# Experts' remainders in halves and quarters of a block: 19 steps a phase for 20

## The chip, the cores and the metric

One core of one Trainium2 chip. The metric is the device time of one execution in microseconds (us); the kernel before takes 680.72 us, the median of three runs.

## The reference

Two stages, one after the other. Attention: 4 batches, 8 heads, 1152 keys of 64 numbers; pairs of queries are averaged, so 576 rows a head. Its output, 4 x 576 = 2304 tokens of 512 numbers, goes through a mixture of eight experts, of which each token uses one:

```python
logits = np.einsum('bsd,de->bse', x, w_gate)
local_gate = 1.0 / (1.0 + np.exp(-np.einsum('bsd,de->bse', x, w_local).squeeze(-1)))
...
            fresh_e = int(np.argmax(logits[b, s]))
            if s == 0 or local_gate[b, s] < 0.5:
                e = fresh_e
            else:
                e = prev_e if prev_e >= 0 else fresh_e
...
            h = np.maximum(x[b, s] @ w1[e], 0.0)
            out[b, s] = p[e] * (h @ w2[e])
```

w1 is 512 x 1024 and w2 1024 x 512 for each expert; p is the softmax of the token's logits. How many tokens an expert gets depends on the data.

## The kernel before, in words

Attention runs over 32 heads until about 422 us; the change does not touch it. The gate of the last batch and the routing follow, and then the experts.

**Blocks.** Tokens are sorted by expert into blocks of 128. A phase has `NST` = 20 steps, one block each. 16 of them hold tokens of one expert (whole blocks). The four of `PAIRS` = (7, 11, 15, 19) hold two halves of 64 tokens, each with an expert of its own: the part of an expert's tokens that is left over its whole blocks goes into a half if it is at most 64, else into a whole block. `positions` (L1045) gives a pair two positions, j and one from 25 on. Where more than 16 whole blocks are needed, five further blocks are computed by `tail` (L1226) behind a branch.

**Phases.** There are eight: w1's quarter q in phase 2q (`mm1`, `block1`), w2's quarter q in phase 2q + 1 (`mm2`, `block2`). All numbers are split into a high and a low half of 16 bits, so each product is three matmuls. W[0] and W[1] hold the current quarter of w1 and of w2 for all eight experts. While a phase runs, the other one's W is filled for the next phase: 16 pieces, each loaded by SP (`w_load`, 256 KB), its high half made by ScalarE (`w_hi`, L586), its low half by VectorE (`w_lo`, L592). In step j of phases 1 to 6 the load of piece c goes out at j = 14c // 15, the high half three steps later, the low half four. Seven buffers hold loads.

**mm1.** The stationary operand is a 128 x 128 piece of the block's weights, the moving one the 128 tokens; a whole block has 24 matmuls of 128 columns, a pair 48 of 64. Since the expert is known only at run time, its 512 KB of weights (128 x 2048) are copied out of W first (`copy`, L1048): by VectorE into one of three `wc` buffers, or by a DMA of SP into one of three `wd` buffers (`DMAC` names the step and the position). VectorE's copies are issued one step ahead, SP's four steps ahead but never across a phase. The result goes through ScalarE (L1071: relu, high half of h) and VectorE (L1072: low half of h).

**mm2.** The stationary operand is h, the moving one 512 columns of the expert's weights, read in W[1] itself through a register; a whole block has 6 matmuls. A pair writes its halves to PSUM partitions 0 to 63 and 64 to 127 by 12 matmuls on 64 columns of the array each; the second half's weights come from a `wd` copy. In phase 1 ScalarE takes the result into `acc` (L1125), later VectorE adds to it (L1129), and in phase 7 GpSimd scatters each block's rows to the output (L1220).

**The order of work** is written out by hand: the instructions of each engine run in the program's order, and `experts` (L1100) issues, step by step, the copies, in phase 0 the gathers and transposes of later blocks, the halves of W, then the matmuls. SP's queue has the loads and the wd copies in that one order.

**Routing.** The first six blocks (`NF`) are settled from three batches and computed for phase 0 while the last batch is routed. Then `route_ops` (s1 to s9, L881 to L957) does some 25 small operations on VectorE: counts, a running sum over the experts, block and row of each token; 40 matmuls (L934, L936) turn them into lists of token numbers, by which GpSimd gathers the blocks (L1019). The list `rest` (L785) weaves these with the gate's and with the first blocks' work (`PLAN`).

```python
DMAC = {5: 0, 7: 1, 9: 0, 11: 1, 13: 0, 15: 1, 17: 0, 19: 1}
...
        elif DMAC.get(j) == k and ph:
            w, src, eng = self.wd.tile([128, 2048], F16, name="wd", tag="wd"), self.es[c], self.nc.sync.dma_start
...
            copy_to(byd, min(i + 4, ph * NST + NST - 1))
            copy_to(byv, min(i + 1, ph * NST + NST - 1))
```

Of the kernel before, what the change touches and what calls it, by code (L numbers as in the profile page):

```python
# [442 lines left out]
NBLK = 25  # L443
NST = 20
PAIRS = (7, 11, 15, 19)
NFULL = NST - len(PAIRS)
NCOL = NBLK + len(PAIRS)
PST = slice(PAIRS[0], NST, 4)
NG = 20
# [17 lines left out]
DMAC = {5: 0, 7: 1, 9: 0, 11: 1, 13: 0, 15: 1, 17: 0, 19: 1}  # L467
# [4 lines left out]
def consts():  # L472
# [7 lines left out]
    full = [j for j in range(NBLK) if j not in PAIRS]  # L480
    key = np.zeros(NCOL)
    key[full] = np.arange(len(full))
    key[list(PAIRS) + list(range(NBLK, NCOL))] = len(full) + np.arange(2 * len(PAIRS))
    a[:, 384:384 + NCOL] = key[None]
    c["c16"] = a
    f = np.zeros((128, 113), np.float32)
    f[:, 0:8] = 8 - np.arange(8)
    f[:, 8:16] = np.arange(8)
    f[:, 16:32] = 1
    f[:, 24] = 0  # L490
    f[:, 34:59] = np.where(np.isin(np.arange(NBLK), PAIRS), 99, key[:NBLK])
    f[:, 60:85] = 4000 + np.arange(128)[:, None] * 25 + np.arange(25)[None]
# [23 lines left out]
class Moe:  # L516
    def __init__(self, tc, ctx, cc, io, out):
# [12 lines left out]
        self.c32 = per.tile([128, 113], F32, name="c32")  # L530
# [12 lines left out]
        self.eji = per.tile([128, NCOL], I32, name="eji")  # L543
# [7 lines left out]
        self.ejf = per.tile([128, NCOL], F32, name="ejf")  # L551
# [43 lines left out]
    def gate_ops(self, b, XR, xT, sml, psum, ptag, wide):  # L595
# [199 lines left out]
    def full_ops(self, sml, psum, ptag):  # L795
# [76 lines left out]
    def route_ops(self):  # L872
# [8 lines left out]
        def s1():  # L881
# [6 lines left out]
            st["ni"], st["en"] = w[:, 216:232].bitcast(I32), w[:, 232:248]  # L888
            st["s3"] = w[:, 248:308].rearrange("p (g v) -> p g v", v=3)
            st["jf"], st["c"] = w[:, 308:328], w[:, 328:348]  # L890
            V.tensor_scalar(out=st["ni"][:, 0:8], in0=self.cy, scalar1=63.0, scalar2=None, op0=ALU.add)
            V.tensor_scalar(out=st["ni"][:, 8:16], in0=self.cy, scalar1=127.0, scalar2=None, op0=ALU.add)

        def s2():
            V.tensor_scalar(out=st["ni"], in0=st["ni"], scalar1=7, scalar2=None, op0=ALU.arith_shift_right)
            V.tensor_copy(st["vec"][:, 8:24], st["ni"])
            V.tensor_tensor(out=st["vec"][:, 16:24], in0=st["vec"][:, 16:24], in1=st["vec"][:, 8:16], op=ALU.subtract)

        def s3():
# [22 lines left out]
        def s8(psum, ptag):  # L922
# [9 lines left out]
            for h in (1, 0):  # L932
                for g in range(h * hg, h * hg + hg):
                    T.matmul(p2, self.R[:, g], jj[:, g, :, 0:n], start=(g == hg), stop=False, skip_group_check=True)  # L934
                for g in range(h * hg, h * hg + hg):
                    T.matmul(p2[64:128, :, PAIRS[0] - NF:NST - NF:4], self.R[:, g, 0:64], jj[:, g, :, n:nc_], start=False, stop=(g == hg - 1), skip_group_check=True)  # L936
            ge, ej = w[:, 0:8 * n].rearrange("p (j e) -> p j e", e=8), self.ejf[:, NF:NBLK]
            gh, eh = w[:, 152:216].rearrange("p (j e) -> p j e", e=8), st["c"][:, 0:8]
            V.tensor_tensor(out=ge, in0=c32[:, 34 + NF:59].unsqueeze(2).to_broadcast(bj), in1=en[:, 0:8].unsqueeze(1).to_broadcast(bj), op=ALU.is_ge)
            V.tensor_tensor(out=gh, in0=c32[:, 8:16].unsqueeze(2).to_broadcast(be), in1=en[:, 8:16].unsqueeze(1).to_broadcast(be), op=ALU.is_ge)  # L940
            V.tensor_reduce(out=ej.unsqueeze(2), in_=ge, op=ALU.add, axis=AX.X)
            V.tensor_reduce(out=eh.unsqueeze(2), in_=gh, op=ALU.add, axis=AX.X)

        def s9():
            pi, en, w = st["pi"], st["en"], st["w2"]
            ej, t1, eh = self.ejf[:, NF:NBLK], self.cnt, st["c"][:, 0:8]
            V.tensor_scalar(out=self.gid[:, NF:], in0=pi[:, n:2 * n], scalar1=1152.0, scalar2=None, op0=ALU.add)
            V.tensor_tensor(out=ej, in0=ej, in1=self.E1[:, NF:], op=ALU.add)
            V.tensor_copy(self.ejf[:, PST], eh[:, 0:4])
            V.tensor_copy(self.ejf[:, NBLK:], eh[:, 4:8])  # L950
# [3 lines left out]

            V.tensor_copy(self.nbi, en[:, 7:8])
# [4 lines left out]
            def b0():  # L960
                V.tensor_copy(self.ejf[64:128, PST], self.ejf[64:128, NBLK:])
# [431 lines left out]
```

## Time and profile before

| | |
|---|---|
| runs | 680.72 us median (679.49 to 680.77, three runs) |
| the profiled execution | 675.04 us, of which the span is 672.9 |
| TensorE (PE) | 642.0 us busy, 95% of the span |
| VectorE (DVE) | 552.1 us, 82% |
| ScalarE (ACT) | 428.1 us, 64% |
| GpSimd (POOL) | 421.4 us, 63% |
| mean granted TensorE clock | 0.984 of 2.4 GHz |
| moved by DMA | 128.80 MB, 191 GB/s over the span |

Start times in rows count from the span's start; the phases begin at 447.67 (phase 0, from its seventh block), 474.88, 501.68, 528.77, 555.57, 582.67, 609.46 and 636.56 us. A busy share is an average over a stretch, and what a stage waits for is read in that stage. PE is the matmuls, PEld the loads of their stationary operand, SPq the queue on which SP issues DMAs: a row of it shows the issue, not the transfer. Matmul rows show a duration longer than the distance of two starts, since matmuls overlap in the array; the distance is what one costs.

### The profile page before, as it was taken

How to read it: one execution, taken by the hardware profiler on the slowest of the kernel's cores; microseconds unless marked ns; L12 is line 12 of the kernel's file. 1: busy time of each engine (PE TensorE's matmuls, PEld its weight loads, DVE VectorE, ACT ScalarE, POOL GpSimd, SP SyncE). 2: the span in 40 equal slices, each digit the busy share in tenths (PEclk: the TensorE clock that was granted, in tenths of full speed). 3: DMA queues.
4: the chain of work that ended last, by engine and by line, in shares of the span. 5: the costliest groups of instructions: out<-in, count | busy, mean ns of one | idle time of the engine just before them, and what ended most of it. 6: DMA issues, size and time to landing. Idle time of an engine off the chain costs nothing.

```text
span 672.9 us, 22880 instructions
## 1 busy us (share of the span) xinstructions
PE 642.0 (95%) x9247; PEld 499.0 (74%) x9247; DVE 552.1 (82%) x1045; ACT 428.1 (64%) x846; POOL 421.4 (63%) x383
## 2 busy tenths in 40 slices
PE   7999999999999999999999998789999999999994
PEld 2587888888888888878887787679559649848941
DVE  7788897897998888898888897759559899899852
ACT  3678778777778677778677565559776535544500
POOL 8899999998898998898998758166000000000064
PEclk9899999999999999999999999789999999999998
DMA  8864654667474578473684307678669769777763
GB/s 245 198 173 148 201 152 111 188 163 161 140 220 113 164 180 160 139 241 90 200 181 126 108 2 133 222 236 255 208 232 325 260 237 304 287 266 260 268 235 121
DMA packets 83228, 128.80 MB, mean 191 GB/s; under 512 B 35759, under 2 KB 42031, under 8 KB 83120
## 3 DMA queue, kind: packets, MB, share of 16 engines
q1 hardware_dynamic: 79920, 117.24, 58.7%
q0 software_dynamic: 3200, 10.05, 4.3%
q8 instruction: 76, 1.25, 0.7%
q14 instruction: 32, 0.26, 0.1%
HBM read 68.82 MB, written 10.04 MB: 117 GB/s over the span
## 4 chain that ended last, share of the span: by engine, by line
PE 51%; issue 29%; DVE 10%; POOL 4%; ACT 2%; DMA 2%; another core or an unknown queue 0%; SPq 0%; POOLq 0%; DVEq 0%; ACTq 0%
PE sc L268 9%; PE sc L270 8%; PE psm L242 7%; PE av L308 6%; PE av L311 5%; PE av L310 5%; PE av L312 4%; DVE mx L244 4%; POOL out L1220 3%; DVE pl L284 2%; PE psh L257 1%; PE psh L1205 1%; PE psm L240 1%; DMA xT<-xr 1%; DVE w L592 1%
## 5 line engine op out<-in xcount | busy, mean ns | idle before, releaser
L272 ACT ACTIVATE ph<-sc 128x576 f32<-128x576 f32 x288 | 186.9, 652 | 91.8 <-PE sc L270 72.9
L244 DVE TENSOR_REDUCE mx<-psm 128x1 f32<-128x512 f32 (+1 forms) x300 | 194.1, 663 | 44.4 <-PE psm L242 41.0
L284 POOL TENSOR_TENSOR pl<-ph 128x576 f16<-128x576 f32 x167 | 207.1, 1256 | 9.0 <-ACT ph L272 9.0
L312 PE MATMUL av<-vt,pl 128*128 128x65 f16 x1235 | 138.2, 192 | 1.1 <-issue 1.1
L311 PE MATMUL av<-vt,ph 128*128 128x64 f16 x1235 | 139.1, 195 | 0.0
L310 PE MATMUL av<-vt,ph 128*128 128x65 f16 x1235 | 138.6, 193 | 0.0
L311 PEld LDWEIGHTS <-ph 128*128 128x128 bf16 x1235 | 115.3, 97 | 20.6 <-issue 0.3
L1220 POOL DMA_INDIRECT out<-acc,sid x14 | 13.7, 979 | 177.6 <-DVE acc L1129 175.4
L310 PEld LDWEIGHTS <-ph 128*128 128x128 bf16 x1235 | 116.4, 97 | 10.9 <-issue 2.9
L268 PE MATMUL sc<-qs,ks 128*128 128x288 f16 x576 | 118.0, 286 | 2.8 <-DVE st L718 1.0
L270 PE MATMUL sc<-qa,ks 65*128 65x288 f16 (+1 forms) x576 | 118.1, 286 | 0.6 <-ACT qa L258 0.6
L312 PEld LDWEIGHTS <-pl 128*128 128x128 f16 x1235 | 115.7, 99 | 1.3 <-issue 1.3
L1216 PE MATMUL pso<-w,hq 128*128 x480 | 107.4, 380 | 0.0
L592 DVE SCALAR_TENSOR_TENSOR w<-wf,w 128x512 f16<-128x512 f32 x124 | 94.3, 765 | 13.1 <-ACT w L586 12.8
L1205 PEld LDWEIGHTS <-wc 128*128 128x128 f16 x1728 | 89.2, 99 | 7.2 <-issue 6.6
L1216 PEld LDWEIGHTS <-hq 128*128 128x128 f16 (+1 forms) x576 | 45.8, 102 | 59.8 <-issue 11.7
L586 ACT ACTIVATE w<-wf 128x512 f16<-128x512 f32 x124 | 76.4, 626 | 18.0 <-DMA wf<-wq 17.8
L1205 PE MATMUL psh<-xr,wc 128*128 128x128 f16 (+1 forms) x1584 | 85.0, 212 | 1.5 <-ACT xr L1034 0.7
L242 PE MATMUL psm<-ks,qs 128*128 128x512 f16 x232 | 83.2, 379 | 0.6 <-DVE mx L244 0.6
L284 DVE TENSOR_TENSOR pl<-ph 128x576 f16<-128x576 f32 x80 | 82.4, 1030 | 1.2 <-issue 1.2
L270 PEld LDWEIGHTS <-ks 65*128 65x128 f16 (+1 forms) x576 | 56.5, 98 | 15.4 <-issue 0.8
L1071 ACT ACTIVATE hq<-psh 128x256 f16<-128x256 f32 x74 | 28.4, 384 | 52.4 <-PE psh L1205 51.6
(241 smaller groups left out, 1014.5 us busy)
## 6 DMA issues: line engine op xcount, KB each, us to landing
wf<-wq SPq DMA_DIRECT2D x124, 256.0 KB
wd<-w SPq DMA_DIRECT2D x40, 512.0 KB
ks<-kd SPq DMA_DIRECT2D x32, 288.0 KB
vf<-vL SPq DMA_DIRECT2D x16, 576.0 KB
qf<-qeo SPq DMA_DIRECT2D x15, 576.0 KB
kf<-kT SPq DMA_DIRECT2D x14, 576.0 KB
qs<-qh SPq DMA_DIRECT2D x60, 72.0 KB
ks<-kl SPq DMA_DIRECT2D x30, 144.0 KB
```

Of the source, the lines that this page charges most:

```text
L242: T.matmul(m[:, 0:w], q[:, t * 128:t * 128 + 128], k[:, c * 512:c * 512 + w], start=True, stop=True)
L244: V.tensor_reduce(out=mx[:, i, c:c + 1], in_=m[:, 0:w], op=ALU.max, axis=AX.X)
L268: T.matmul(sc[:, c, 0:288], ksl, QS[p][:, j, c * 288:(c + 1) * 288], start=True, stop=False)
L270: T.matmul(sc[:, c, 0:288], kal, QA[p % 3][u, j, c * 288:(c + 1) * 288], start=False, stop=True)
L272: A.activation(out=PHI[g % NPH][:, r * Q:(r + 1) * Q].rearrange("p (c q) -> p c q", c=2), in_=sc[:, :, 0:288], func=AF.Exp, scale=1.0 / 16)
L284: x.tensor_tensor(out=PLO[g % NPH][:, r * Q:r * Q + Q], in0=pf, in1=top(pf), op=ALU.subtract)
L310: T.matmul(o, ph[:, c:c + 128], v[:, j, kt, 0:65], start=(kt == 0 and t == 0), stop=False, skip_group_check=True)
L311: T.matmul(o[:, 0:64], ph[:, c:c + 128], v[:, j, kt, 65:129], start=False, stop=False, skip_group_check=True)
L312: T.matmul(o, pl[:, c:c + 128], v[:, j, kt, 0:65], start=False, stop=(kt == NKT - 1 and t == 4), skip_group_check=True)
L592: self.nc.vector.scalar_tensor_tensor(out=lo, in0=t, scalar=float(2 ** (W2S if ph % 2 else W1S)), in1=hi, op0=ALU.mult, op1=ALU.subtract)
L1205: self.nc.tensor.matmul(p[:, ft, c], u[:, ws, kk, ft * 128:ft * 128 + 128], x[:, 2 * kk + xs_, c], start=(n == 0 and ft == 0 and i == 0), ...
L1216: self.nc.tensor.matmul(p[c], h(hs, ft)[:, c], u(ws, ft), start=(first and n == 0), stop=(last and n == e), skip_group_check=(m < 128))
```

## The change

Halves are joined by quarters. A phase has 19 steps: 16 whole blocks, two of halves (8 and 13) and one of four quarters (18). A remainder up to 32 tokens goes into a quarter, one up to 64 into a half, and what finds no room among four halves and four quarters into a whole block. The step of quarters has four positions, so 96 matmuls of 32 columns in mm1 and 24 on 32 columns of the array in mm2. The routing gets a third rounding, a longer scan, and 80 matmuls more for the quarters' lists. `DMAC` is a list now, with three of the quarters' four weight copies by DMA, in phase 0 too, so a first-matrix phase has eight copies by DMA as before (three in phase 0, where it had none), a second-matrix phase five for four; VectorE still copies 16 times in phases 2, 4 and 6.

```diff
-NBLK = 25
-NST = 20
-PAIRS = (7, 11, 15, 19)
-NFULL = NST - len(PAIRS)
-NCOL = NBLK + len(PAIRS)
+NBLK = 24
+NST = 19
+PAIRS = (8, 13)
+QUAD = 18
+SPEC = PAIRS + (QUAD,)
+NFULL = NST - len(SPEC)
+NCOL = NBLK + 6
...
-DMAC = {5: 0, 7: 1, 9: 0, 11: 1, 13: 0, 15: 1, 17: 0, 19: 1}
+DMAC = ((4, 0), (6, 0), (8, 1), (10, 0), (13, 1), (18, 1), (18, 2), (18, 3))
...
-            V.tensor_scalar(out=st["ni"][:, 0:8], in0=self.cy, scalar1=63.0, scalar2=None, op0=ALU.add)
-            V.tensor_scalar(out=st["ni"][:, 8:16], in0=self.cy, scalar1=127.0, scalar2=None, op0=ALU.add)
+            V.tensor_tensor(out=st["ni"].rearrange("p (v e) -> p v e", v=3), in0=self.cy.unsqueeze(1).to_broadcast([128, 3, 8]),
+                            in1=c32[:, 114:138].rearrange("p (v e) -> p v e", v=3), op=ALU.add)
...
-            V.tensor_tensor_scan(out=st["en"], data0=c32[:, 16:32], data1=st["vec"][:, 8:24], initial=self.F, op0=ALU.mult, op1=ALU.add)
+            hq, es, ov = st["hq"][:, 9:26], st["es"][:, 0:17], st["ov"]
+            V.tensor_tensor_scan(out=es, data0=c32[:, 16:33], data1=hq, initial=0.0, op0=ALU.mult, op1=ALU.add)
+            V.scalar_tensor_tensor(out=ov[:, 9:26], in0=es, scalar=4.75, in1=hq, op0=ALU.is_gt, op1=ALU.mult)
+            V.tensor_reduce(out=st["vec"][:, 8:16].unsqueeze(2), in_=ov.rearrange("p (v e) -> p e v", v=3)[:, 0:8], op=ALU.add, axis=AX.X)
+            V.tensor_tensor_scan(out=st["en"], data0=c32[:, 85:93], data1=st["vec"][:, 8:16], initial=self.F, op0=ALU.mult, op1=ALU.add)
...
+            for g in range(NG):
+                for c in range(4):
+                    T.matmul(pq[32 * c:32 * c + 32, 0:2], self.R[:, g, 0:32], jj[:, g, :, n + 2 + c], start=(g == 0), stop=(g == NG - 1), skip_group_check=True)
...
+            V.tensor_scalar(out=self.gid[:, QUAD:QUAD + 1], in0=st["pq"][:, 1:2], scalar1=1152.0, scalar2=None, op0=ALU.add)
+            V.tensor_copy(t1[:, QUAD - NF:QUAD - NF + 1], st["pq"][:, 0:1])
             V.tensor_copy(self.nbi, en[:, 7:8])
...
-        return [j, NBLK + PAIRS.index(j)] if j in PAIRS else [j]
+        return [j, NBLK + PAIRS.index(j)] if j in PAIRS else [j, NBLK + 5, NBLK + 6, NBLK + 7] if j == QUAD else [j]
...
-        elif DMAC.get(j) == k and ph:
+        elif (j, k) in DMAC and (ph or j == QUAD):
...
-            if j in PAIRS:
-                wd = self.wcp.pop((i, 1))
-                w.append(lambda s, ft: wd[:, s * 1024 + ft * 512:s * 1024 + ft * 512 + 512])
+            for k in range(1, len(self.positions(j))):
+                wd = self.wcp.pop((i, k))
+                w.append(lambda s, ft, wd=wd: wd[:, s * 1024 + ft * 512:s * 1024 + ft * 512 + 512])
...
-        first = [NF - 2 + c if c < NE else NF + (c - NE) * 10 // 11 for c in range(16)]
+        first = [NF - 2 + c if c < NE else NF + (c - NE) * 9 // 11 for c in range(16)]
...
-        byd = [(i, k) for i, k in parts if i > NST and DMAC.get(i % NST) == k and (k or i // NST % 2 == 0)]
+        byd = [(i, k) for i, k in parts if (i > NST or i % NST == QUAD) and (i % NST, k) in DMAC and (k or i // NST % 2 == 0)]
```

## Rows read from the trace of the kernel before

**Rows 1.** Busy time by stretch: phases 0, 1, 2, 3, 4 and 7; x counts instructions.

```profile
core 0: us, PE busy (x) PEld busy (x) DVE busy (x) ACT busy (x) POOL busy (x), PEclk, DMA share, GB/s
447.67:474.88 27.21, 26.41 (x528) 25.69 (x528) 24.61 (x52) 23.62 (x40) 15.61 (x21) 0.95 0.67 205
474.88:501.68 26.80, 26.80 (x150) 11.44 (x147) 13.90 (x22) 21.50 (x36) 0.00 (x0) 1.00 0.66 228
501.68:528.77 27.09, 27.09 (x578) 27.09 (x577) 24.12 (x48) 16.31 (x36) 0.00 (x0) 1.00 0.93 320
528.77:555.57 26.80, 26.80 (x150) 11.42 (x147) 24.47 (x38) 10.02 (x17) 0.00 (x0) 1.00 0.69 235
555.57:582.67 27.10, 27.10 (x579) 27.10 (x578) 25.52 (x51) 15.64 (x35) 0.00 (x0) 1.00 0.90 313
636.56:663.40 26.84, 26.84 (x150) 11.41 (x146) 14.14 (x20) 0.38 (x1) 15.66 (x16) 1.00 0.57 218
```

**Rows 2.** Timeline of TensorE in phase 4: start, duration, line, operands, shape, count.

```profile
562.28 1.50 PE L1205 MATMUL psh<-xr,wd 128*128 128x128 f16 x24
563.62 1.85 PE L1205 MATMUL psh<-xr,wc 128*128 128x128 f16 x36
...
566.36 1.50 PE L1205 MATMUL psh<-xr,wc 128*128 128x128 f16 x24
```

**Rows 3.** The gate's matmuls: the source line L661 (ns min/median/max), and its timeline.

```profile
L661 PE MATMUL wide<-wgh,xT x120: 167/169/184, 159.4 to 353.3; 128*128 128x18 f16 x60, 128*128 128x9 f16 x60
...
159.44 1.15 PE L661 MATMUL wide<-wgh,xT 128*128 128x18 f16 x40
```

**Rows 4.** Timeline of TensorE in phases 1 and 3.

```profile
474.88 5.34 PE L1216 MATMUL pso<-w,hq 128*128 x24
...
538.17 0.38 PE L1216 MATMUL pso<-w,hq 128*64 x1
538.17 0.38 PE L1216 MATMUL pso<-wd,hq 128*64 128x512 f16 x1
...
539.35 4.39 PE L1216 MATMUL pso<-w,hq 128*128 x19
...
544.76 4.39 PE L1216 MATMUL pso<-w,hq 128*128 x19
```

**Rows 5.** Timeline of phase 2: VectorE, and TensorE's weight load of step 16.

```profile
522.59 0.70 DVE L1062 COPY wc<-w 128x2048 f16 x1
...
523.34 1.34 PEld L1205 LDWEIGHTS <-wc 128*128 128x128 f16 x24
...
524.12 0.70 DVE L592 SCALAR_TENSOR_TENSOR w<-wf,w 128x512 f16<-128x512 f32 x1
```

**Rows 6.** SP's queue: issues around phases 2 and 4, and what they waited for.

```profile
SPq L1062 <- DVE w L592: 32.1, 6, 6.4
...
499.77 0.49 SPq L1062 DMA_DIRECT2D wd<-w  x1
...
509.92 0.49 SPq L1062 DMA_DIRECT2D wd<-w  x1
...
553.08 0.49 SPq L1062 DMA_DIRECT2D wd<-w  x1
```

**Rows 7.** Timeline of ScalarE: the high half of piece 14, in phases 2 and 4.

```profile
524.63 0.63 ACT L586 ACTIVATE w<-wf 128x512 f16<-128x512 f32 x1 [0.74 <-DMA wf<-wq]
...
577.87 0.63 ACT L586 ACTIVATE w<-wf 128x512 f16<-128x512 f32 x1
```

**Rows 8.** Timeline of the routing: VectorE and TensorE.

```profile
431.77 0.17 DVE L895 TENSOR_SCALAR wf<-wf 128x16 int32<-128x16 int32 x1
431.97 0.17 DVE L896 CAST wf<-wf 128x16 f32<-128x16 int32 x1
...
436.97 0.48 PE L936 MATMUL pi<-wf,R 128*64 128x8 f16 x10
...
442.44 1.38 PE L1205 MATMUL av<-xr,wc 128*128 128x128 f16 x19 [0.99 <-DVE wc L1062]
```

**Rows 9.** Timeline of GpSimd: the last scatter.

```profile
667.37 0.98 POOL L1220 DMA_INDIRECT out<-avf,sid  x1 [0.31 <-issue]
```

More of the change, by code (lines that the diff above doesn't have):

```diff
@@ L479, in consts @@
     a[:, 256:384] = 1
-    full = [j for j in range(NBLK) if j not in PAIRS]
-    key = np.zeros(NCOL)
+    full = [j for j in range(NBLK) if j not in SPEC]
+    key = np.full(NCOL, 999.0)
     key[full] = np.arange(len(full))
-    key[list(PAIRS) + list(range(NBLK, NCOL))] = len(full) + np.arange(2 * len(PAIRS))
+    key[list(PAIRS) + [NBLK, NBLK + 1]] = len(full) + np.arange(4)
+    key[NBLK + 2:] = len(full) + 0.5 + np.arange(4)
     a[:, 384:384 + NCOL] = key[None]
     c["c16"] = a
-    f = np.zeros((128, 113), np.float32)
+    f = np.zeros((128, 146), np.float32)
     f[:, 0:8] = 8 - np.arange(8)
     f[:, 8:16] = np.arange(8)
-    f[:, 16:32] = 1
+    f[:, 16:33] = 1
     f[:, 24] = 0
-    f[:, 34:59] = np.where(np.isin(np.arange(NBLK), PAIRS), 99, key[:NBLK])
-    f[:, 60:85] = 4000 + np.arange(128)[:, None] * 25 + np.arange(25)[None]
+    f[:, 34:34 + NBLK] = np.where(np.isin(np.arange(NBLK), SPEC), 99, key[:NBLK])
+    f[:, 60:60 + NBLK] = 4000 + np.arange(128)[:, None] * 25 + np.arange(NBLK)[None]
+    f[:, 114:138] = np.repeat([63, 95, 127], 8)[None]
+    f[:, 138:146] = np.array([2, 3, 0, 1, 0.5, 1.5, 2.5, 3.5])[None]
     f[:, 85:93] = 1
@@ L529, in __init__ @@
         self.c16 = con.tile([128, 640], F16, name="c16")
-        self.c32 = per.tile([128, 113], F32, name="c32")
+        self.c32 = per.tile([128, 146], F32, name="c32")
         self.wgf = con.tile([128, 4, 9], F32, name="wgf")
@@ L542, in __init__ @@
         self.sid = per.tile([128, NBLK], U32, name="sid")
-        self.eji = per.tile([128, NCOL], I32, name="eji")
+        self.eji = per.tile([128, NBLK + 8], I32, name="eji")
         self.nbi = per.tile([128, 1], I32, name="nbi")
@@ L550, in __init__ @@
         self.pall = per.tile([128, NST], F32, name="pall")
-        self.ejf = per.tile([128, NCOL], F32, name="ejf")
+        self.ejf = per.tile([128, NBLK + 8], F32, name="ejf")
         self.cnt = per.tile([128, NBLK - NF], F32, name="cnt")
@@ L932, in s8 @@
             for h in (1, 0):
[L933 removed]
+                gs = range(h * hg, h * hg + hg)
+                for g in gs:
                     T.matmul(p2, self.R[:, g], jj[:, g, :, 0:n], start=(g == hg), stop=False, skip_group_check=True)
[L935 to L936 removed]
+                for g in gs:
+                    T.matmul(p2[64:128, :, PAIRS[0] - NF:PAIRS[1] + 1 - NF:PAIRS[1] - PAIRS[0]], self.R[:, g, 0:64], jj[:, g, :, n:n + 2], start=False, stop=(g == hg - 1), skip_group_check=True)
```

62 lines of the change are left out of this document (36 added, 26 removed).

## The prediction

> **What bounds the kernel now.** I read the stretches first, since the change touches the routing (about 430 to 447 us) and the eight expert phases behind it. From 474.88 us on TensorE is busy for the whole of every stretch at a granted clock of 1.00 (2.4 GHz); in phase 0 it is busy 26.41 of 27.21 us [rows 1]. So a step that goes is worth what it holds of TensorE, if nothing else then decides. Two things nearly do, in the first-matrix phases (2, 4 and 6) alone: the DMA share is 0.93 and 0.90, and VectorE is busy 24.1 to 25.5 of 27.1 us. In the second-matrix phases (1, 3, 5, 7) the share is 0.66 to 0.69 and VectorE has room. The attention in front is not touched. The sum is made against the profiled execution (675.04 us, span 672.9); the median of the runs is 5.68 above it, no term below hangs on that, so the difference is taken from 680.72.
>
> **Does it compute the same blocks?** The experts get 192, 447, 145, 124, 34, 656, 132 and 574 tokens of the reference's inputs. Remainders over 64 go up to a whole block: 15 + 1 = 16 wholes, the old and the new limit. Before, 64, 63, 34, 62, 17, 16 and 4 are seven halves; after, the first four are halves (room for 4) and the last three quarters (room for 4). It fits exactly; no tail block runs.
>
> **TensorE's steps.** First matrix: a whole step runs from 562.28 to 563.62, 1.34; from 563.62 to 566.36 stand a whole and a pair, so the pair is 1.40 (48 matmuls of 64 columns, 29 ns each) [rows 2]. A step of quarters has 96 matmuls of 32 columns, each on a fresh 128x128 weight. No such row exists. Above stands 29 ns (2.80 us), below 32/64 of the pair's (1.40). Nearest is the gate's group of 9 and 18 columns with 128x128 weights: 40 in 1.15 us, the last one's 0.17 off, is 25 ns [rows 3]. I take 25: 2.41 us. Phase before: 16 x 1.34 + 4 x 1.40 = 27.1, as the stretch says; after: 21.46 + 2.80 + 2.41 = 26.7, a gain of only 0.4.
>
> Second matrix: 24 matmuls take 5.34, the last one's 0.38 off: 0.216 each, so a whole step of six is 1.29; three wholes and a pair take 544.76 - 539.35 = 5.41, so a pair is 1.53 [rows 4]. Its two halves start at the same 538.17: both column tiles run at once, and 0.24 goes at the change of shape. For four tiles I take the same, 1.53; bounds: 1.29, and if only two ran at once 12 x 0.216 + 0.24 = 2.83. Phase: 26.8 before, 16 x 1.294 + 3 x 1.53 = 25.3 after, a gain of 1.5. The Trainium skill (TensorE: Matmul & The Clock Gate, "Measured speedup vs the span model") measured 2.38 times for three column tiles, not 3; by that efficiency four tiles give 3.17 times, an estimate of 24 x 0.216 / 3.17 + 0.24 = 1.87 a step and 1.4 us less gain over four phases. The row's two tiles lose nothing, and no run here has three, so the sum stays.
>
> **DMA and VectorE in phases 2, 4, 6.** VectorE does 16 weight copies, as before, but after step 10 they now come in eight steps running. One round of copy, low half and the remainder of h (L1062, L592, L1072) is 524.12 - 522.59 = 1.53 against a step of 1.34, and the copy begun at 522.59 (done 523.29) already let TensorE's loads start only at 523.34 [rows 5]. Eight rounds lag by 8 x 0.19 = 1.5; how much of it copies made early take up, no row shows (0 to 1.5). I take 0.8, the middle: floor 26.7 + 0.8 = 27.5.
>
> The transfers weigh more. Both versions move 8 weight copies of 512 KB and 16 loads of 256 KB, 32 units of 256 KB, per such phase; at a share of 0.90 they ran at 313 GB/s, so 347 at full share, 0.755 us a unit, 24.2 in all [rows 1]. Before, the first two loads were fetched in the phase ahead, the first copy was issued at 499.77 and 553.08, 1.9 and 2.5 us before the phase began (as soon as the last half of W was written: SP's copies wait for DVE L592 six times, 32.1 us), and the last copy stood behind the last load [rows 1, 6]. After, the copy for step 4 stands ahead of every load in SP's program, and its buffer is one that the quarters of step 18 just held: it cannot go before the phase begins, the loads queue behind it, and the three copies of step 18 (issued at step 14; the third waits for step 13) stand before the last load. So all 32 units run between the phase's start and the last load's landing. The overhead: from 499.77 to 524.63, when ScalarE got load 14, is 24.86 for 27 units (20.4), in phase 4 553.08 to 577.87 is 24.79 [rows 6, 7]. 4.4 to 4.5 remain; shares of 0.93 and 0.90 put 1.9 and 2.7 of idle into them at most (one is the wait for step 5's buffer, 509.92), which leaves 1.7 to 4.5. I take 3.0, near the lower end, since the new order has no such idle: load 15 lands at 27.2. Its high half (0.63, rows 7) and low half (0.70) make W complete at 28.5, and the next phase reads W by a register, so it waits for all of it. Bounds 27.5 (the floor) and 30.0. Each phase grows by 28.5 - 27.1 = 1.4 where TensorE's sum gave -0.4; the steps in between wait for late loads, which lies inside this. In the second-matrix phases the third quarter copy holds load 15 back too: step 14 begins at 18.5, three units take 2.3, some 2 more to land; 0.63, 0.70 and VectorE's first copy of 0.70 end at 24.9, just inside 25.3.
>
> **Routing.** VectorE gains about three dependent small operations net (scan, threshold, sum), 0.2 each by the distance of two starts (431.77, 431.97): +0.65 before the indices [rows 8]. TensorE gains 80 matmuls of 2 columns behind the old forty: at 25 ns 2.0 [rows 3], at 48 (ten of the half form in 0.48) 3.8, a quarter if four tiles overlap. Behind them stand the transpose of block 5 and the matmuls of blocks 3 to 5; block 5 waited 0.99 at 442.44, and that much is cover. VectorE's two copies of the new columns wait for the 80 too, behind the old ones, and with them its copy for step 6. Bounds: 0, were all of it covered, and 0.65 + 3.8 - 0.99 = 3.5; I take +1.5, near the middle.
>
> **Phase 0.** Thirteen steps for fourteen: 10 x 1.34 + 4 x 1.40 and 13 gathered blocks' transposes (8 of the size of a whole step's 24 matmuls, 0.45) were 24.9; 13.4 + 2.8 + 2.41 + 12 x 0.45 are 24.0: -0.9. Three DVE copies become DMAs, share 0.67: nothing more.
>
> **End.** TensorE ends at 663.40 but GpSimd issues the last scatter only at 667.37, each 0.98 with 0.31 ahead of it [rows 1, 9]; one scatter fewer: -1.3 for phase 7.
>
> **Sum.** Routing +1.5, phase 0 -0.9, phases 1, 3 and 5 -1.5 each, 2, 4 and 6 +1.4 each, 7 -1.3: **-1.0 us**, 679.7. A measurement of this kernel tells 0.2% (1.36 us) from nothing, so this stands near the bound.
>
> **Rivals.**
> A, the sum above: own range 677.2 to 682.2 (0.5 us a phase for the landing, 1 for the routing). Chance 0.45.
> B, transfers keep up: landings come within 1 us of the last byte, and the floor of 27.5 decides. The three phases then cost +0.4 each, 3.0 less: 676.7. For it: TensorE never waited for a wd tile. Against: share 0.93 already. Chance 0.25. The Trainium skill (DMA: Bandwidth & Descriptors, Specifications) gives 435 GB/s for the fabric, which would bring B about; the 347 at full share speak against it.
> C, slower: the four column tiles of the quarters run only two at a time. Place: step 18 of phases 1, 3, 5, 7; price 1.30 each, 5.2: 684.9. It decides once the step passes 1.8 us (4 x 0.25 eats the 1.0). Against: the pair overlaps fully. Chance 0.12.
> D, the front: TensorE's 80 matmuls and the columns behind them hold up the gathers and block 5 by the full 3.5, 2.0 more: 681.7, no change that can be told. Chance 0.15.
> E, a count above 16 wholes on the chip brings five tail blocks, each with 4 MB to load (12 us by 347 GB/s): far above 690. The trace has no tail now. Chance 0.03.
>
> **Numbers.** A lies about half beyond 0.2% faster (0.23), else mostly within (0.17; slower 0.05); B is faster; D is 0.02 faster, 0.08 the same, 0.05 slower; C and E are slower. Faster 0.50, same 0.25, slower 0.25. The range 675.5 to 683.5 leaves out C, E and B's edge.
>
> **What would show it.** A: stretches of phases 2, 4, 6 of 28 to 29 us with DMA share above 0.93 and TensorE idle in them, the quarter step at 2.4 us; phases 3 and 5 at 25.3; phase 0 about 26.3 and beginning 1.5 later. B: phases of 27.5 without waits for wf or W. C: 24 matmuls of step 18 over 2.8 us. The forecast is wrong if the first-matrix phases are shorter than 27.1, or if the quarters' matmuls are not at 25 ns.

## The result, and the profile after

**Slower.** After: 682.83 us, the median of 20 runs (678.56 to 689.77); before, beside it: 679.53 (20 runs, 673.49 to 687.67). Ratio 1.0071 [1.0048, 1.0094], so +4.8 us where -1.0 was forecast: the direction was wrong. (The ratio leaves out the slow executions; the medians alone differ by 3.3.) The time lies inside my range of 675.5 to 683.5, which was wide enough for either direction. The profiled execution took 688.53 us (span 686.7), 13.5 above that of before; 8.0 of it lies ahead of the last batch's token column, in attention, whose code is the same (the column begins at 429.85 in the trace of before and at 437.88 in this one). Single executions differ there by several us (E13 and E14 below), so I compare stretches of the traces.

Busy time by stretch, phases 0 to 7 of after (columns as in rows 1):

```profile
459.40:487.58 28.18, 24.44 (x521) 23.73 (x521) 23.74 (x52) 22.52 (x38) 11.61 (x17) 1.00 0.69 237
487.58:512.96 25.38, 25.33 (x151) 10.85 (x147) 12.17 (x19) 20.82 (x35) 0.00 (x0) 1.00 0.63 218
512.96:542.35 29.39, 28.36 (x577) 26.79 (x578) 25.21 (x49) 15.73 (x35) 0.00 (x0) 1.00 0.93 333
542.35:567.61 25.26, 25.26 (x150) 10.87 (x147) 22.98 (x36) 9.79 (x17) 0.00 (x0) 1.00 0.65 220
567.61:596.12 28.51, 28.10 (x581) 26.79 (x578) 25.97 (x51) 15.17 (x34) 0.00 (x0) 1.00 0.93 343
596.12:621.38 25.26, 25.26 (x150) 10.87 (x147) 22.98 (x36) 9.89 (x17) 0.00 (x0) 1.00 0.65 219
621.38:651.20 29.82, 28.42 (x580) 26.83 (x577) 26.17 (x51) 15.22 (x34) 0.00 (x0) 1.00 0.78 284
651.20:676.45 25.25, 25.25 (x151) 10.82 (x147) 12.28 (x18) 0.38 (x1) 14.21 (x15) 1.00 0.65 248
```

Against [rows 1]: phases 1, 3, 5 give 1.4 to 1.5 each, as forecast; phases 2, 4, 6 cost 2.3, 1.4 and 2.7, where I had 1.4 each; phase 0 costs 1.0 where I had -0.9. The eighth row, phase 7, gives 1.6 to its last matmul.

TensorE's timeline of after: the step of quarters in phase 2, its first and its last two groups in phase 3, and the routing.

```profile
540.25 1.05 PE L1231 MATMUL psh<-xr,wd 128*128 128x32 f16 x36
541.15 0.45 PE L1231 MATMUL psh<-xr,wc 128*128 128x32 f16 x12
541.45 1.05 PE L1231 MATMUL psh<-xr,wd 128*128 128x32 f16 x36
542.35 1.89 PE L1242 MATMUL pso<-w,hq 128*128 x8
...
566.20 0.40 PE L1242 MATMUL pso<-wd,hq 128*32 128x512 f16 x3
...
567.08 0.38 PE L1242 MATMUL pso<-w,hq 128*32 x1
567.08 0.39 PE L1242 MATMUL pso<-wd,hq 128*32 128x512 f16 x3
567.29 0.38 PE L1242 MATMUL pso<-w,hq 128*32 x1
567.29 0.39 PE L1242 MATMUL pso<-wd,hq 128*32 128x512 f16 x3
...
446.84 0.77 PE L957 MATMUL pq<-wf,R 128*32 128x2 f16 x80
448.00 2.98 PE L1231 MATMUL av<-xr,wc 128*128 128x128 f16 x48
454.76 2.21 PE L1231 MATMUL av<-xr,wc 128*128 128x128 f16 x24 [3.78 <-DVE hq L1098]
```

36 matmuls of 32 columns take 0.90 from start to start (540.25 to 541.15), 25 ns each, and the step 96 x 25 = 2.4. In phase 3 the four column tiles start together every 0.21, as two did in [rows 4], and the step takes 1.41 (566.20 to the stretch's end at 567.61). Two things are new: TensorE stands 3.78 us in the routing, and in phase 2 the engines wait longer for loads. The waits in phase 2, after and then before (engine, line, what for: us in total, times, longest):

```profile
ACT w L591 <- DMA wf<-wq: 5.8, 5, 2.4
PEld L1231 <- DVE wc L1088: 2.2, 8, 0.5
PEld L1231 <- DMA wd<-w: 0.9, 2, 0.7
```

```profile
ACT w L586 <- DMA wf<-wq: 1.0, 2, 0.7
PEld L1205 <- DVE wc L1062: 0.4, 1, 0.4
```

SP's queue at the start of phase 2 of after:

```profile
512.94 0.49 SPq L1088 DMA_DIRECT2D wd<-w  x1
513.48 2.73 SPq L586 DMA_DIRECT2D wf<-wq  x3
```

The first copy goes at 512.94, the phase's start, where that of before went at 499.77, 1.9 ahead of it [rows 6]; the loads stand behind it. This much is as forecast. But it is not the end of W that decides: its last low half is written at 541.41, 28.45 into the phase (I had 28.5), and TensorE's own steps end only at 29.39.

```profile
540.73 0.68 DVE L597 SCALAR_TENSOR_TENSOR w<-wf,w 128x512 f16<-128x512 f32 x1
```

### The profile page after: what moved, and what is told of

Its sections match the earlier page's. It is cut to its first block, busy times and chain, and to the rows that moved or that the text cites. A ratio compares the mean times of both kernels' runs of the same rounds, so it can differ in the third digit from the quotient of the medians.

```text
span 686.7 us, 23006 instructions
## 1 busy us (share of the span) xinstructions
PE 645.3 (94%) x9319; PEld 498.3 (73%) x9319; DVE 553.1 (81%) x1043; ACT 424.8 (62%) x840; POOL 415.3 (60%) x380
## 4 chain that ended last, share of the span: by engine, by line
PE 68%; DVE 14%; DMA 6%; issue 4%; POOL 2%; ACT 2%; SPq 1%; another core or an unknown queue 1%; DVEq 1%; POOLq 0%; ACTq 0%
PE pso L1242 13%; PE sc L268 9%; PE sc L270 8%; PE psh L1231 8%; PE psm L242 6%; PE av L308 5%; PE av L311 4%; PE av L310 4%; PE av L312 4%; DVE mx L244 4%; DMA wf<-wq 3%; DVE pl L284 2%; DMA xT<-xr 2%; DVE w L597 1%; PE psh L257 1%
## 5 line engine op out<-in xcount | busy, mean ns | idle before, releaser
L1242 PE MATMUL pso<-w,hq 128*128 (+2 forms) x456 | 101.3, 380 | 0.0
L1231 PEld LDWEIGHTS <-wc 128*128 128x128 f16 x1656 | 87.4, 99 | 15.9 <-issue 9.7
L1231 PE MATMUL psh<-xr,wc 128*128 128x128 f16 (+2 forms) x1512 | 85.1, 212 | 4.9 <-DVE hq L1098 1.6
L284 DVE TENSOR_TENSOR pl<-ph 128x576 f16<-128x576 f32 x80 | 85.3, 1067 | 1.1 <-issue 1.1
L1242 PEld LDWEIGHTS <-hq 128*128 128x128 f16 (+2 forms) x576 | 43.5, 99 | 55.9 <-issue 8.0
L308 PEld LDWEIGHTS av<-vx,ph 128*128 128x128 f32 x410 | 51.9, 191 | 5.8 <-issue 3.2
```

The source lines that it names most:

```text
L284: x.tensor_tensor(out=PLO[g % NPH][:, r * Q:r * Q + Q], in0=pf, in1=top(pf), op=ALU.subtract)
L1231: self.nc.tensor.matmul(p[:, ft, c], u[:, ws, kk, ft * 128:ft * 128 + 128], x[:, 2 * kk + xs_, c], start=(n == 0 and ft == 0 and i == 0), ...
L1242: self.nc.tensor.matmul(p[c], h(hs, ft)[:, c], u(ws, ft), start=(first and n == 0), stop=(last and n == e), skip_group_check=(m < 128))
```

## The experiments

Run n is En. Three theories of where the loss comes from are tested. Theory 1: the order of SP's queue makes the transfers of phases 2, 4 and 6 late. Theory 2: VectorE's rounds (copy, low half, h) of 1.53 us pace the steps there. Theory 3: the loss lies in the front, the gate and routing of the last batch.

The timings fall into two kinds: before has medians of 670.4 to 672.2 beside E1 to E12 (one run of 669.6 beside E18), and of 679.0 to 679.5 beside the first timing and E13 to E17; I call them A and B. Whether the chip makes the kind is not shown: chip number 6 stands beside E13 to E15 (B) and beside E18 (A). "Front" runs from the token column's first matmul to phase 0, "front and phase 0" on to phase 1.

**E1**, before once more.

> The kernel before, unchanged, profiled a second time, to see which stretches repeat. Theory 1 (the loss is made in the first-matrix phases and, a little, in the front) expects the phases to repeat within 0.05 us (27.1 and 26.8) and the front, from the first matmul of the last batch's token column to phase 0, at 17.8 again, with phase 0 at 27.2. Rival (front and attention differ from execution to execution, the change costs nothing there) expects the front anywhere between 17.8 and 21.5 and the total time of the stretch before it to move by several us.

673.19 us, kind A. Phases 1 to 6 repeat to 0.01 us; front and phase 0 take 42.71 where the first trace (kind B) has 45.03, phase 7 and the end 33.94 for 36.35. So phases 1 to 6 of before can be compared between single traces, the rest only within a kind.

**E2**, after with half loads (the line of the load is shown; `w_hi` and `w_lo` read `t[:, 0:256]` twice).

```diff
-        self.nc.sync.dma_start(out=t, in_=self.io["wq"][ph, c // 2, :, (c % 2) * 512:(c % 2) * 512 + 512])
+        self.nc.sync.dma_start(out=t[:, 0:256], in_=self.io["wq"][ph, c // 2, :, (c % 2) * 512:(c % 2) * 512 + 256])
```

> The kernel after with every load of experts' weights cut to its first half (128 KB for 256), read twice by ScalarE and VectorE, so their work stays and the weights are wrong. Theory 1 (transfers pace phases 2, 4 and 6, as forecast): the 32 units shrink to 24, the loads land 4 us earlier, and the phases fall from 29.4, 28.5, 29.8 to 27.5 or less, the quarters' step following a gap-free run. Theory 2 (VectorE paces: rounds of copy, low half and h of 1.53 us from step 9 to 17, 0.2 over a step each): phases 2 and 6 fall to 28.5, where phase 4 stands already, as only the waits for wf and wd at steps 7 and 8 go; phase 4 stays at 28.5. Second-matrix phases 25.3 by both.

670.50 us; phases 2, 4 and 6 take 27.56, 27.56 and 27.57. This is theory 1's number; phase 4, which theory 2 left at 28.5, fell too.

**E3**, after without the low halves of h in steps 10 to 17, VectorE's work.

```diff
-            return f[3]
+            return None if i // NST in (2, 4, 6) and 10 <= i % NST < 18 else f[3]
```

> The kernel after without the low half of h in steps 10 to 17 of phases 2, 4 and 6 (24 VectorE instructions of 0.33 us left out; the output is wrong there), so VectorE's round is 1.20 us instead of 1.53, under a step of 1.34. Transfers and copies stay as they are. Theory 2 (VectorE paces): steps 14 to 17 go at 1.34 instead of 1.55, phase 4 falls from 28.5 to 26.9, phases 2 and 6 from 29.4 and 29.8 to about 27.8 and 28.2. Theory 1 (transfers pace): TensorE waits for the late halves of W instead, the phases stay within 0.3 of 29.4, 28.5, 29.8.

672.66 us; the phases take 27.75, 28.35 and 28.01. Phases 2 and 6 fall by 1.6 and 1.8 as theory 2 said, phase 4 by 0.2 as theory 1 said; steps 14 to 17 do go at TensorE's pace (1.34 each, read as in E4 below). So neither theory holds alone: less to transfer (E2) and less work on VectorE (E3) each shorten the phases. I read it as one behind the other: a late load makes VectorE start its run of rounds late, and VectorE, which works 25 to 26 us of such a phase, has too little slack to make that up.

**E4**, after with SP's copies issued three steps ahead instead of four, one number.

```diff
-            copy_to(byd, min(i + 4, ph * NST + NST - 1))
+            copy_to(byd, min(i + 3, ph * NST + NST - 1))
```

> The kernel after with SP's copies issued three steps ahead instead of four, one number: loads 0 and 1 now stand before the first copy in SP's program and load 15 before the quarters' three copies. Theory 1 (the order of the transfers paces): W is complete about 3 us earlier, phases 2, 4 and 6 fall to 27.5, in all 5.2 us, and the kernel comes out level with or just under the one before (ratio 0.997 to 1.001). Theory 2 (VectorE's rounds pace): phases 2 and 6 lose the waits at steps 7 and 8 and come to 28.5, phase 4 stays at 28.5, in all 2.2 us (ratio about 1.004).

667.45 us, ratio 0.9964 [0.9932, 0.9996]: a little faster than before. The phases take 27.55, 27.56 and 27.55, theory 1's number. That is also the floor of 27.5 that I had worked out for VectorE, and TensorE's timeline of phase 4 shows it at work: steps 14 to 17 take 6.46 from start to start, less 0.30 for the quarters' first twelve matmuls in the same row, so 1.54 each, VectorE's round.

```profile
571.77 6.61 PE L1231 MATMUL psh<-xr,wc 128*128 128x128 f16 x108
578.23 1.05 PE L1231 MATMUL psh<-xr,wd 128*128 128x32 f16 x36
```

**E5** and **E6**, the two moves of E4 apart: in E5 only the first copy goes behind loads 0 and 1, in E6 only the quarters' copies go behind load 15.

```diff
-            copy_to(byd, min(i + 4, ph * NST + NST - 1))
+            copy_to(byd, min(i + 4 - (j == 0), ph * NST + NST - 1))
```

```diff
-            copy_to(byd, min(i + 4, ph * NST + NST - 1))
+            copy_to(byd, min(i + 4 - (j == QUAD - 4), ph * NST + NST - 1))
```

> The kernel after with the first copy of a first-matrix phase alone issued three steps ahead (loads 0 and 1 before it in SP's program); the quarters' three copies stay ahead of load 15. Run 4 showed that both moves together bring phases 2, 4 and 6 from 29.4, 28.5, 29.8 to 27.55. If the copy at the phase's start is what costs (loads 0 and 1 prefetched, 6 units of 256 KB less ahead of each later load), the three phases come to 27.6 to 27.8 here. If the quarters' copies ahead of load 15 cost (my prediction's reason for W being complete at 28.5), they stay above 28.3.

> The other half of the edit of run 4: the quarters' three copies one step later, behind load 15, the first copy left ahead of load 0. If the first copy costs, phases 2, 4 and 6 stay at 28.5 to 29.8 with waits for wf around steps 4 to 9; if the quarters' copies cost, they come to 27.6. The second-matrix phases stay at 25.3 in either case.

E5: 673.91 us, phases 27.56, 27.56, 27.56. E6: 677.57 us, phases 30.21, 28.50, 30.90. The whole cost hangs on the first copy; the quarters' copies ahead of load 15 cost nothing. Phase 2 by stretch, of E5 and of E6:

```profile
506.56:534.12 27.56, 27.47 (x576) 26.71 (x577) 24.85 (x49) 16.02 (x35) 0.00 (x0) 1.00 0.95 335
```

```profile
503.20:533.41 30.21, 28.58 (x577) 26.79 (x578) 25.23 (x49) 15.56 (x35) 0.00 (x0) 1.00 0.91 324
```

and ScalarE's waits for loads in it, of E5 and of E6:

```profile
ACT w L591 <- DMA wf<-wq: 2.0, 3, 0.8
```

```profile
ACT w L591 <- DMA wf<-wq: 6.7, 5, 2.1
```

The kernel's bytes are the same in both, and the rate nearly so (335 and 324 GB/s). So at the same amount the order alone makes or takes away the cost; fewer bytes take it away too (E2).

W's end follows VectorE's rounds. In E5 the quarters' copies still stand ahead of load 15, and the last low half is written at 533.19, 26.63 into phase 2 and 0.93 before its end; in after it was 28.45 and 0.94:

```profile
532.49 0.70 DVE L597 SCALAR_TENSOR_TENSOR w<-wf,w 128x512 f16<-128x512 f32 x1
```

**E7**, E4 without the quarters' copies in phase 0 (the line in `experts` is shown; `mm1` takes the first quarter's weights four times). It asks what the wait ahead of step 14 of phase 0 is, 1.62 in E4, which no trace of before has.

```diff
-        parts = [(i, k) for i in range(NF + 1, NS) for k in range(len(self.positions(i % NST)))]
+        parts = [(i, k) for i in range(NF + 1, NS) for k in range(1 if i == QUAD else len(self.positions(i % NST)))]
```

> The kernel of run 4 with the three DMA copies of the quarters' weights in phase 0 left out (all four quarters of phase 0 use the first one's weights, so the output is wrong). TensorE's instructions stay the same. In all four traces with the new steps TensorE stands still 1.0 to 1.7 us ahead of step 14 of phase 0, which no trace of before has, and phase 0 takes 26.4 to 28.2 where its own work is 24.1. Theory: the three copies (1.5 MB) in the queues hold up what TensorE waits for there; then the gap falls under 0.3 and phase 0 to 25.2 or less. Rival: the gap belongs to the place in TensorE's program (its sequencer, whatever the transfers do); then it stays at 1.0 or more and phase 0 at 26 or more.

668.23 us; the wait ahead of step 14 is 0.63, and phase 0 takes 25.45 for E4's 26.38. This lies between the two expectations: some 1 us is the copies', 0.6 stays. Phases 2, 4 and 6 take 27.81, 27.56 and 28.02.

**E8**, E4 and one more copy by DMA.

```diff
-DMAC = ((4, 0), (6, 0), (8, 1), (10, 0), (13, 1), (18, 1), (18, 2), (18, 3))
+DMAC = ((4, 0), (6, 0), (8, 1), (10, 0), (13, 1), (15, 0), (18, 1), (18, 2), (18, 3))
```

> The kernel of run 4 with one more copy of a whole block, step 15's, by DMA in phases 2, 4 and 6 (15 copies on VectorE for 16, 0.60 us less in the run of steps that it paces; 9 by DMA, 1.5 us more of transfers). If VectorE's back-to-back rounds of 1.53 us make the 0.85 that is left over TensorE's 26.7, steps 14 to 17 get 0.4 to 0.6 back, phases 2, 4 and 6 come to 27.0 to 27.2, and the kernel is 1 to 1.5 us under run 4 (ratio about 0.994). If the transfers have no room for it (34 units less the 2 prefetched, 0.755 each), W is late or TensorE waits for a wd tile, and the phases stay at 27.5 or grow to 28.5 (ratio 0.996 to 1.001).

667.29 us, ratio 0.9913 [0.9884, 0.9943]; phases 28.12, 27.67, 27.05. Both expectations came in part: the later steps go at 1.34, but TensorE waits for wd, 1.03 in phase 2 and 0.54 in phase 4.

**E9**, after again.

> The kernel after, unchanged, timed and profiled again beside the next kernels. From stretches of single traces the change is worth: front +1.2, phase 0 +0.7, phases 1, 3 and 5 -4.5, phases 2, 4 and 6 +6.4, phase 7 and the end -1.3, together +2.5 us, a ratio of about 1.004; the first timing gave 1.0071 [1.0048, 1.0094]. If the stretches tell all, the ratio comes out at 1.003 to 1.006 here, with phases 2, 4 and 6 at 28.4 to 30.9 and the wait ahead of step 14 of phase 0 at 1 to 2 us again; if attention in front also got slower by the new program, it stays at 1.007 or above with the phases the same.

672.58 us for 672.10, ratio 1.0011 [0.9981, 1.0040], kind A; phases 30.15, 28.68, 29.02. The ratio is under the 1.003 to 1.006 that I expected, and not the first timing's 1.0071.

**E10**, a fourth wd buffer.

```diff
-NWD = 3
+NWD = 4
```

> The kernel after with four wd buffers for three, its order unchanged: the first copy of phases 2, 4 and 6 then takes a buffer that was free since step 13 and no longer one that the quarters of step 18 hold to the phase's end. If the hold by the buffer is what makes the first copy cost (it cannot go before the phase begins, and all loads queue behind it), it now goes when W is complete, 0.5 to 2 us before the phase, and phases 2, 4 and 6 fall to 27.6 to 28.0 (ratio 0.995 to 1.000). If the mere place ahead of load 0 costs, they stay above 28.3 (ratio above 1.002).

667.91 us, ratio 0.9934 [0.9901, 0.9966]; phases 28.50, 28.15, 28.11, the first copy issued at 496.71, 0.72 ahead of phase 2. The five traces with the first copy ahead of load 0 and three buffers (after, E6, E9, E13 and E18) have 29.3 in the mean of 15 phases, this one 28.25 and E5 27.56. So roughly 1.0 of the 1.7 is the buffer that step 18 holds, the rest the place ahead of load 0; the 15 phases lie between 27.8 and 30.9, so one trace splits it only roughly.

**E11**, before, its first copy one step earlier.

```diff
-DMAC = {5: 0, 7: 1, 9: 0, 11: 1, 13: 0, 15: 1, 17: 0, 19: 1}
+DMAC = {4: 0, 7: 1, 9: 0, 11: 1, 13: 0, 15: 1, 17: 0, 19: 1}
```

> The kernel before with the copy of step 4 by DMA in place of step 5's, so that it stands ahead of load 0 in SP's program, as in the kernel after; its buffer is free (the last pairs of the phase ahead hold the two others). If the place in the queue alone costs, phases 2, 4 and 6 rise from 27.09 to 28 or more here too; if the hold by the quarters' buffers is needed for the cost, they stay within 0.4 of 27.1, with the first copy issued up to 2 us before the phase.

673.75 us; the phases take 27.50, 27.50 and 27.99 for 27.09. So the place, with the step that changes hands, costs 0.4 to 0.9 in before too, with a free buffer (its first copy goes at 498.34, 1.90 ahead of phase 2).

**E12**, E5, E8 and E10 together.

> The kernel after with the first copy behind loads 0 and 1 (run 5), step 15's copy by DMA (run 8) and four wd buffers, so that the copies for steps 10 and 18 are not late as they were in run 8 (TensorE waited 1.03 and 0.54 there). If VectorE's rounds make the last 0.85 and only late wd copies spoiled run 8, phases 2, 4 and 6 come to 26.9 to 27.2 and the kernel to a ratio of 0.988 to 0.993, under run 8 or level with it. If the transfers have no more room, waits for wd or wf come back and the phases stay at 27.5 to 28.1 (ratio 0.992 to 0.997).

666.01 us (6 runs), ratio 0.9898 [0.9846, 0.9949], kind A: 6.9 us under before by the ratio. The phases take 26.96 each, at DMA shares up to 1.00. Here are phase 4 by stretch, and TensorE's steps 14 to 17 of phase 2, 1.39 each by the reading of E4:

```profile
554.99:581.95 26.96, 26.95 (x581) 26.71 (x578) 25.19 (x50) 15.25 (x34) 0.00 (x0) 1.00 1.00 360
```

```profile
521.77 1.51 PE L1231 MATMUL psh<-xr,wc 128*128 128x128 f16 x24
523.12 1.50 PE L1231 MATMUL psh<-xr,wd 128*128 128x128 f16 x24
524.46 3.31 PE L1231 MATMUL psh<-xr,wc 128*128 128x128 f16 x60
527.62 1.05 PE L1231 MATMUL psh<-xr,wd 128*128 128x32 f16 x36
```

**E13** and **E14**, after and before a third time; **E15**, E12 with the quarters' copies of phase 0 eight steps ahead instead of four.

```diff
-            copy_to(byd, min(i + 4 - (j == 0), ph * NST + NST - 1))
+            copy_to(byd, min(i + (4 - (j == 0) if ph else 8), ph * NST + NST - 1))
```

> The kernel after, unchanged, a third timing with a trace. Stretches of single traces give +2 us (front and phase 0 +1.5, phases 1 to 6 +2.1, phase 7 and the end -1.5 to -2): a ratio of 1.002 to 1.004. If the program also slows the attention in front, as the first trace would have it, the last batch's token column begins 3 us or more later than in the traces of before (429.9 to 432.7) and the ratio is 1.006 or more; if that differs by execution and chip, it begins between 427 and 434 for either kernel.

> The kernel before, unchanged, a third trace: phases 1 to 7 as in rows 1 within 0.05, phase 0 without a wait of 1 us or more ahead of step 14, front and phase 0 together 42.5 to 45.0 (42.71 and 45.03 so far), the token column between 427 and 434. If the front and phase 0 of before are not shorter than those of after (43.1 to 49.7, middle 44.8), the +1.5 put down to them falls.

> The kernel of run 12 with the quarters' three copies of phase 0 issued at step 10 instead of 14, so that the 1.5 MB go through the queues earlier. If they cause TensorE's wait ahead of step 14, it moves to a step between 10 and 13 or goes (under 0.8 at step 14), and phase 0 comes to 25.5 or less if it goes. If the place in TensorE's program causes it, 1.0 us or more stays at step 14. Phases 2, 4 and 6 at 26.96 as in run 12 by both.

E13: 682.44 us, ratio 1.0053 [1.0025, 1.0081] (+3.6 us [1.7, 5.5]), kind B; phases 29.75, 28.36, 29.82; front and phase 0 50.52. Its profiled execution, 687.14 us, is the longest of its 12. E14: 679.54 us, front and phase 0 46.04. The column begins at 434.77 and 433.25. So a loss of the first timing's size comes back in another timing of kind B, and most of what B has over A lies in the front (theory 3; the rest is at the end). Its mark is the wait of 3.8 us. TensorE, ScalarE and VectorE in the routing of E13:

```profile
445.25 3.09 PE L1231 MATMUL av<-xr,wc 128*128 128x128 f16 x48
452.10 1.92 PE L1231 MATMUL av<-xr,wc 128*128 128x128 f16 x24 [3.77 <-DVE hq L1098]
...
450.93 0.38 ACT L1097 ACTIVATE hq<-av 128x256 f16<-128x256 f32 x1 [4.46 <-remote]
...
450.93 0.69 DVE L1088 COPY wc<-w 128x2048 f16 x1 [5.51 <-remote]
```

and TensorE's same blocks in E14 and, of kind A, in E9:

```profile
442.36 2.84 PE L1205 MATMUL av<-xr,wc 128*128 128x128 f16 x48
446.23 1.45 PE L1205 MATMUL av<-xr,wc 128*128 128x128 f16 x20 [1.03 <-DVE wc L1062]
448.01 0.22 PE L1205 MATMUL av<-xr,wc 128*128 128x128 f16 x1 [0.32 <-issue]
```

```profile
439.30 6.29 PE L1231 MATMUL av<-xr,wc 128*128 128x128 f16 x72
```

In E13 ScalarE and VectorE start at one instant, 2.6 after TensorE's rows before them are over, released by nothing the profile shows ("remote"). All seven traces of kind B, before's two too, have such "remote" rows, and none of the 13 of kind A has one.

E9's 6.29 has no wait in it, but it is not the work alone: the granted clock was 0.50 (1.2 GHz) from 436.9 to 443.7, and 40 of the 72 matmuls come 107 ns apart there. E8, whose clock stayed at 2.4 GHz there, takes 4.21 for the 72, at 56 ns each. TensorE had stood 1.72 us just before the fall in E9, and 1.70 at the same place in E8, which has none. The front of E9, the fall in it, and the front of E8 (columns as in rows 1):

```profile
428.17:448.00 19.83, 16.52 (x307) 15.90 (x308) 12.86 (x60) 10.85 (x22) 7.26 (x12) 0.78 0.67 221
436.90:443.70 6.80, 6.80 (x150) 6.72 (x147) 2.87 (x14) 1.41 (x2) 4.00 (x5) 0.50 0.91 293
```

```profile
432.63:449.68 17.05, 13.66 (x307) 12.80 (x308) 12.85 (x60) 10.86 (x22) 5.31 (x8) 0.97 0.69 234
```

E15: 680.24 us, kind B, the wait ahead of step 14 of phase 0 is 0.69, phases 26.95, 26.96, 26.96; front and phase 0 50.23, with the wait in the routing (3.88).

**E16**, E15 timed; **E17**, E2 again; **E18**, after with 4 of the 80 quarter matmuls (each starting and stopping its own sum).

```diff
-            for g in range(NG):
+            for g in range(1):
```

> The kernel of e15 timed: four wd buffers, first copy behind loads 0 and 1, step 15's copy by DMA, the quarters' copies of phase 0 issued at step 10. By stretches against before: phases 1 to 6 -4.9, phase 0 about 0, front +1.2, phase 7 and the end -1.5 to -2 on a chip where before takes 670 to 672 us: -5 to -6 us, ratio 0.990 to 0.993. On a chip where before takes 679 us and the routing stands still 3.8 us longer: -1 to -3 us, ratio 0.995 to 0.999.

> The kernel of run 2 (all loads of experts' weights cut to their first half, read twice; weights wrong) once more, for the routing. On a chip where before takes 679 us: if the wait of 3.8 us ahead of the third block's matmuls behind the routing hangs on the transfers beside it (five loads of 256 KB and the gathers), it shrinks under 2.5 us with loads of 128 KB; if it hangs on the instructions alone, it stays at 3.5 to 4.0. On a chip where before takes 670 to 672 us it is absent as in run 2, and this tells nothing of it; phases 2, 4 and 6 are 27.56 again in either case.

> The kernel after with 4 of the 80 matmuls for the quarters' lists (the first group of tokens only), so the quarters' lists, and with them the output rows of their tokens, are wrong; 152 instructions less for TensorE in the routing. The 80 take 0.77 us, so block 5's matmuls begin 0.7 us earlier relative to the token column, and phase 0 as well where nothing else waits (the front at about 17.6 on a chip where before takes 671 us). On a chip where before takes 679 us: if the added instructions make the wait of 3.8 us ahead of the third block behind the routing, it falls to what the traces of before show there (gaps of 0.3 to 1.0); if not, 3.5 us or more stay.

E16: 677.33 us, ratio 0.9973 [0.9943, 1.0003], kind B, the wait in the routing 4.66; front and phase 0 48.47. E17, kind B: 682.69 us, the wait 4.01, no shorter with loads of half the bytes; phases 27.88, 27.56, 27.56. E18 came out as kind A (670.20 us), where the wait is absent anyway, and so says nothing of it; its wait ahead of step 14 of phase 0 was 0.56, so in this one trace that wait hangs on TensorE's program as well as on the copies.

## Why the prediction was wrong

The measured change was +4.8; the stretches of single traces add up to +6.1 on kind B, the kind of the first timing (see Sum). Between my -1.0 and that lie 7.1 us: 4.1 in the routing and phase 0, 2.3 in phases 2, 4 and 6, and 0.7 at the end. The steps that failed are the routing's +1.5, which had no row for a wait of 3.8 us (its place is shown, its cause is open), and the +1.4 for each of phases 2, 4 and 6, which took the larger of two chains where they add.

- **Blocks, TensorE's steps, second-matrix phases: right.** 2.4 for the quarters' step, 25.26 for 25.3; C is out. The trace goes with the row of two tiles, and not with the Trainium skill's 2.38 times for three column tiles (TensorE: Matmul & The Clock Gate, "Measured speedup vs the span model"): the step took 1.41, not the 1.87 estimated from it.
- **Phases 2, 4 and 6: the late transfers right, the load that is late and the sum wrong.** "I take 3.0 ... load 15 lands at 27.2 ... W complete at 28.5" took the larger of two chains. That W was complete at 28.45 is luck: the quarters' copies ahead of load 15, which made my 28.5, cost nothing (E5), and the last low half comes 0.94 before the phase's end with them or without. What decided was the first copy ahead of the early loads (E5, E6), whose lateness VectorE, at its floor, did not make up: 27.55 plus the wait, 29.3 in the mean. Three phases cost 6.4 to 6.7 (after, E9, E13), not 4.2. VectorE's floor of 27.5 was right (E2, E4, E5), and one copy less on VectorE brings it down (E12); its 0.8 over TensorE's 26.7 had been the middle of 0 to 1.5, so the exact size was luck too. B's condition, transfers that keep up, came true once the order was mended, not in this kernel.
- **Routing: near on A, wrong on B.** The 80 matmuls took 0.77 (9 ns each: four tiles overlap), inside my bounds. On A, front and phase 0 together are 1.6 longer (middle of nine traces with the new steps, E7 and E18 left out, 44.77; E1 and E11 42.71 and 43.59), on B 4.7 (middle of five 50.23; 45.03 and 46.04), where my terms made +0.6. "+1.5, near the middle" had no row for a wait of 3.8, in all five B traces with the new routing; before on B has a milder one (E14: ScalarE 3.4 us "remote", TensorE in gaps of 0.3 to 1.0). What makes it is open; it is not the bytes of the experts' loads (E17).
- **Phase 0:** "Three DVE copies become DMAs, share 0.67: nothing more" failed. TensorE is busy 24.0 to 24.3 there on A at a granted clock of 1.00 (E7 and E18 left out), the 24.0 worked out, for 25.0 in E1, so the -0.9 of work came; but it stands 1.0 to 2.1 ahead of step 14, of which the copies make about 1 (E7, E15). At a clock of 1.00 phase 0 takes 26.1 to 26.8 on A, for E1's 25.73. My sum for before, 24.9, was also 2.3 under the 27.21 of its row, and I did not ask why: that row has a clock of 0.95, E1's has 1.00. E1 and E9:

```profile
449.67:475.40 25.73, 25.01 (x529) 24.47 (x529) 24.55 (x52) 23.87 (x40) 17.45 (x23) 1.00 0.68 219
```

```profile
448.00:474.56 26.56, 24.18 (x521) 23.61 (x520) 23.82 (x52) 22.66 (x38) 12.86 (x17) 1.00 0.75 258
```

- **End:** -1.3 forecast; -1.6 to -2.4 on A (E9 32.38; E1 33.94, E11 34.83), -0.2 to -0.9 on B.
- **Sum.** On B +4.7 - 4.5 + 6.5 - 0.6 = +6.1: at the upper edge of the first timing's +4.8 [3.3, 6.4] and above E13's +3.6 [1.7, 5.5]. The two profiled executions of after on B were long ones (the second longest of 20 and the longest of 12), so the 4.7 for front and phase 0 is probably too much. On A +1.6 - 4.5 + 6.6 - 2.0 = +1.7, with +0.7 [-1.3, 2.7] measured. Rival D was the nearest in place, some 2 us too small, and not in mechanism, for the 80 matmuls themselves took 0.77.

## What to carry to other kernels

When a queue is shared, ask of its first transfer in a stage what buffer it needs and who holds that; a copy whose buffer is held to the stage's end makes every prefetch behind it late, at equal bytes. Where the next engine in line has no slack, add the delay to its floor; don't take the larger of the two. Time a change of a few us in several sessions before believing it: here its price was 0.1% in one and 0.5 to 0.7% in two others.

## What the runs showed that was not expected

- Sessions differ by more than this change: 670 to 672 us against 679 for the same program. Traces of the second kind have waits of 1 to 5 us that end by nothing shown ("remote", "issue") in the routing and in phase 7, where E13's VectorE stands one of 3.38 us; E1 and E9 have none there.
- Traces of the second kind also lack records: between 400 and 500 us they hold 1100 to 1245 semaphore records, those of the first kind 1519 to 1622, and ahead of 300 us both hold about as many. So "remote" can mean that the releaser's record is missing. Whether the waits and the missing records have one cause, the recording itself perhaps, no run tests.
- The spread of the front on A goes mostly with TensorE's clock. Most traces have one fall to 1.2 GHz of 3.4 us in the routing or in phase 0, before's too, and then front and phase 0 take 44.5 to 44.8 with the new steps and 42.7 to 43.6 without. E8 has no fall and takes 43.13, E3 and E9 have one of 6.8 us and take 46.2 and 46.4, and E5 has two and takes 46.7. E18 does not fit: it has no fall and takes 44.4, standing in phase 0 instead (27.18).
- The weights' transfers can run at a DMA share of 1.00 and 360 GB/s through a whole phase (E12) with TensorE never waiting for them, above the 347 that I had worked out for a full share, though under the 435 GB/s of the Trainium skill (DMA: Bandwidth & Descriptors, Specifications).
